# A conditioned transformer block on one core: the last two attention runs cut into four, gelu in chunks at the end, the residual of the last tile by an identity matmul, and Q projections asked for one group earlier

## The chip, the cores and the metric

The kernel runs on one core of a Trainium2 chip. The metric is device time in microseconds (us), from the start of the program on that core to its end. Five engines work from queues of their own: TensorE (PE: matmuls, PEld: its weight loads), VectorE (DVE), ScalarE (ACT), GpSimd (POOL) and SyncE (SP, which here issues nearly all DMAs). An engine executes its queue in order; between engines there are only semaphores.

## The reference

What is computed, with B = 1, S = 2048 tokens, D = 512, 32 heads of 16, F = 1376, all tensors bf16:

```python
mod = (_silu(c) @ w_mod).reshape(c.shape[0], 6, 1, -1)
sa, ca, ga, sb, cb, gb = (mod[:, 0], ..., mod[:, 5])
h = _layernorm(x) * (1 + ca) + sa
qkv = (h @ wqkv).reshape(B, S, 3, H, Dh)          # q, k, v per head
p = softmax(q @ k^T * Dh ** (-0.5))
x = x + ga * ((p @ v).reshape(B, S, D) @ wo)
h = _layernorm(x) * (1 + cb) + sb
x = x + gb * (gelu_tanh(h @ w1 + b1) @ w2 + b2)
```

## The kernel before

**Tiling.** The 2048 tokens are four query blocks of 512 (`QB`), each of four 128-token tiles. Attention is done in 32 runs (`runs`, `NR`). A run takes four heads side by side and one query block of 512 columns; in the last block (`LAST`) a run takes eight heads and one half of the block, so that 256 columns of two heads stand beside each other. In a run the 16 key tiles of 128 are gone through; one key tile and one of the four head rows make a unit of 128 x 512 scores.

**Two ways to an exponential.** The score matmuls (`qk`, L856) contract over 32 rows and run side by side in row tiles of the PE array. For 12 of the 16 key tiles of a run the exponential is taken by ScalarE (L905), on groups of three and two units in turn (`SPAN = (3, 2)`, so 1536 and 1024 columns). For the other four (`DKS`) VectorE writes the score as an integer that is read as a bf16 (L946), with four shifted copies of it (L962, L978; pieces of the last copy are done by GpSimd, L984), and the five readings are averaged by weighted V. The product with V (`pv_op`, L1044) runs in column tiles of 32 and accumulates a run in one PSUM bank `od`; one row of V is a constant, so the softmax denominator comes with it.

**Order.** Nothing is scheduled on the chip. A list scheduler in the kernel file (`Plan`) gives each operation a duration, priorities (`dyn`) and due times, and writes out each engine's queue in the order that its own clock gives. Small differences between priorities come from a table `SEEDS`, one number for each 25 us of that clock. The order is fixed when the kernel is built.

**Around attention.** In front: x, `w_mod` and `wqkv` are loaded, `mod` for the first norm is made by matmuls with one column (L617, `mod_columns`), block 0 is normalised (`layer_norm`: `stats` on DVE, `rstd` on GpSimd, `apply` on DVE), transposed (L694) and modulated (L657 on ACT, L660 on DVE), then Q, K and V of the first heads are projected (`make_q`, `make_k`, `make_v`). Later Q groups are projected when the scores of the run before them are built (`want_q`, called in `qk_deps`); their rows are spread by eight small DMAs (`qm<-qs`, L763). After each run `normalise` copies `od` to SBUF, sends the denominators through DRAM and multiplies. After the last run of a block `block_tail` does the output projection (`wo_mm`), the second norm, the two matrices of the MLP and the store. ScalarE's gelu needs another table than its exponential, so each block's gelu stands between two table loads.

**The end.** Tiles 0 and 1 of the last block have their first MLP matrix done while the last runs go on; their gelu (L1281) waits until the last exponential is done (`finished`). Tiles 2 and 3 are finished by `last_half` after the last run: division on chip by two 32x32 transposes (L1336 to L1343), output projection, residual (L1353), norm, transposes (L1369), first matrix (L1381), gelu straight from PSUM (L1384), second matrix (L1210), sum (L1396), store.

## Time and profile before

| | us |
|---|---|
| median of 3 runs | 783.46 |
| lowest, highest | 781.15, 783.68 |
| the profiled execution: span from first to last instruction | 782.9 |

The profile's only time for its execution is this span; it lies 0.56 us below the median and inside the three runs. The page gives each engine's busy time, the chain of work that ended last, and groups of instructions by source line. A group is named by its line, engine and operation, with what it writes and reads; "x313" is a count. Timeline rows give start, duration, engine, line, operation, tiles and count, and in brackets the engine's idle time before it and what ended it. Window rows give, for a stretch of time, the busy time of PE, PEld, DVE, ACT and POOL, then the granted clock of PE as a share of full speed, the share of the DMA engines that was busy, and GB/s. A busy PE counts the latency of its matmuls (a 512-column matmul shows 0.38 us, though the next one starts after 0.22 us).

### The profile page before, as it was taken

To read this page: it belongs to the slowest core of one execution; us is meant where nothing else is said; L and a number is where in the kernel's file an instruction comes from. 1 tells how busy PE (TensorE), PEld (TensorE's weight loads), DVE (VectorE), ACT (ScalarE), POOL (GpSimd) and SP (SyncE) were. 2 spreads that over 40 slices of the span, in tenths; PEclk is the share of its full clock that TensorE was granted. 3 is DMA by queue.
4 is the path that set the end of the run, shared out by engine and by line. 5 is a ranking of instruction groups with operands and counts; after the bars stand their busy time and mean duration, and the time that the engine had idled before them with its cause. 6 is when DMAs were issued, how large, how long until landed. Compare 5 with 4: busy or idle time off the path is not lost.

```text
span 782.9 us, 20900 instructions
## 1 busy us (share of the span) xinstructions
PE 730.8 (93%) x8315; PEld 271.3 (35%) x8395; DVE 722.6 (92%) x1269; ACT 752.0 (96%) x677; POOL 256.6 (33%) x492
## 2 busy tenths in 40 slices
PE   8889999999999999999999999999999999999997
PEld 3323333233333222233223233332333444444444
DVE  6789989999999999999999999999987999998984
ACT  4999999999999999999999999999999999999994
POOL 6620434333352534231313134234202432142320
PEclk9999999999999999999999999999999999999999
DMA  7043001100002001000101000000110000100000
GB/s 216 28 147 83 18 23 43 27 23 5 17 21 75 25 17 49 17 13 15 47 19 30 29 19 17 20 22 19 29 57 24 23 22 18 46 25 18 25 18 28
DMA packets 38547, 27.71 MB, mean 35 GB/s; under 512 B 17941, under 2 KB 33846, under 8 KB 38450
## 3 DMA queue, kind: packets, MB, share of 16 engines
q1 hardware_dynamic: 38442, 26.39, 11.8%
q8 instruction: 65, 1.06, 0.5%
q14 instruction: 32, 0.26, 0.1%
q10 hardware_dynamic: 8, 0.00, 0.0%
HBM read 20.77 MB, written 2.61 MB: 30 GB/s over the span
## 4 chain that ended last, share of the span: by engine, by line
ACT 37%; PE 34%; DVE 16%; issue 10%; DMA 2%; POOL 1%; SPq 0%; DVEq 0%; POOLq 0%; ACTq 0%
ACT pt L905 35%; PE od L1044 12%; PE st L856 10%; DVE ph L946 7%; DVE sh L962 4%; PE ax L1210 4%; PE ax L1271 3%; PE ax L856 2%; PE ax L735 1%; DMA blk<-in_w_mod_dram 1%; ACT g L1286 1%; PE t L1381 1%; DVE sh L978 1%; PE od L481 1%; DVE g L1276 1%
## 5 line engine op out<-in xcount | busy, mean ns | idle before, releaser
L905 ACT ACTIVATE pt<-st 128x1536 bf16<-128x1536 f32 x626 | 710.7, 1325 | 7.6 <-PE st L856 3.8
L946 DVE TENSOR_SCALAR ph<-ax 128x512 int16<-128x512 f32 x484 | 315.8, 681 | 25.3 <-PE ax L856 23.1
L856 PE MATMUL st<-qm,kT 32*128 32x512 bf16 x1564 | 246.4, 384 | 26.7 <-ACT pt L905 19.9
L962 DVE TENSOR_SCALAR sh<-ph 128x2048 int16<-128x2048 int16 x363 | 242.4, 700 | 2.0 <-PE od L1044 1.2
L984 POOL TENSOR_TENSOR sh<-ph,pair_sh 128x256 int32<-128x256 int32 x212 | 128.8, 616 | 280.6 <-DVE sh L962 190.4
L1044 PE MATMUL od<-sh,VX 128*32 128x512 bf16 (+1 forms) x2432 | 172.5, 342 | 1.7 <-DVE sh L962 0.7
L856 PE MATMUL ax<-qm,kT 32*128 32x512 bf16 x484 | 165.2, 380 | 7.3 <-DVE ph L946 4.3
L856 PEld LDWEIGHTS <-kT 32*128 32x128 bf16 x2048 | 79.4, 91 | 240.6 <-issue 228.7
L1044 PE MATMUL od<-pt,VEB 128*32 128x512 bf16 (+1 forms) x1952 | 142.7, 342 | 0.7 <-DVE OD L1069 0.5
L1044 PEld LDWEIGHTS <-VX 128*32 128x32 bf16 x2432 | 60.2, 96 | 82.7 <-issue 71.6
L1044 PEld LDWEIGHTS <-VEB 128*32 128x32 bf16 x2560 | 62.9, 96 | 73.5 <-issue 58.9
L1096 POOL TENSOR_TENSOR OT<-OD,RB 128x256 bf16<-128x256 f32 x38 | 29.0, 774 | 72.7 <-DVE sh L962 60.1
L978 DVE TENSOR_SCALAR sh<-ph 128x2048 int16<-128x2048 int16 (+3 forms) x86 | 50.7, 594 | 0.4 <-PE od L1044 0.3
L1044 PE MATMUL od<-ph,VEB 128*32 128x512 bf16 (+1 forms) x608 | 48.5, 341 | 0.4 <-DVE OD L1069 0.4
L1271 PE MATMUL ax<-blk,W 128*128 128x512 bf16 (+1 forms) x155 | 41.5, 352 | 1.7 <-issue 0.5
L1096 POOL TENSOR_TENSOR OS<-OD,RB 128x256 bf16<-128x256 f32 x24 | 17.5, 741 | 63.2 <-DVE sh L962 26.0
L790 POOL TENSOR_SCALAR VX<-VEB 128x128 bf16<-128x128 bf16 x64 | 23.4, 366 | 38.0 <-DVE VEB L667 34.8
L1210 PE MATMUL ax<-w,g 128*128 128x512 bf16 x115 | 32.4, 381 | 2.2 <-ACT g L1281 1.1
L735 PE MATMUL ax<-blk,w 128*128 128x512 bf16 x93 | 30.9, 383 | 2.8 <-ACT blk L657 0.6
L1276 DVE TENSOR_SCALAR g<-ax,b1c 128x512 bf16<-128x512 f32 (+1 forms) x44 | 29.3, 678 | 0.2
L641 DVE BATCH_NORM_STATS2 ln_s<-xb 128x6 f32<-128x512 bf16 x32 | 21.7, 678 | 1.8 <-DMA xb<-in_A_x_dram 1.7
L1210 PEld LDWEIGHTS <-g 128*128 128x128 bf16 x176 | 14.1, 97 | 24.5 <-issue 11.9
(109 smaller groups left out, 407.5 us busy)
## 6 DMA issues: line engine op xcount, KB each, us to landing
RB<-rn SPq DMA_DIRECT2D x124, 64.0 KB
xb<-in_A_x_dram SPq DMA_DIRECT2D x7, 512.0 KB
out_dram<-o SPq DMA_DIRECT2D x16, 128.0 KB
qm<-qs SPq DMA_DIRECT2D x120, 16.0 KB
W<-in_B_w_dram SPq DMA_DIRECT2D x1, 1376.0 KB
w<-in_A_wqkv_dram SPq DMA_DIRECT2D x3, 384.0 KB
blk<-in_w_mod_dram SPq DMA_DIRECT2D x2, 512.0 KB
g<-in_w_mod_dram SPq DMA_DIRECT2D x2, 512.0 KB
```

What stands on the lines that cost most here:

```text
L735: return chain([(lambda ps, j=j: nc.tensor.matmul(out=ps[:, 0:QB], lhsT=w.tile[:, j, cc * P:(cc + 1) * P], rhs=o_h[b].tile[:, j, :], start ...
L856: nc.tensor.matmul(out=o.tile[:, k * QB:(k + 1) * QB], lhsT=kT[cc][kb][rows, ko * P:(ko + 1) * P], rhs=qm.tile[rows, par, :] if hb is None ...
L905: nc.scalar.activation(out=e.tile[:, 0:len(got) * QB], in_=o.tile[:, 0:len(got) * QB], func=ACT.Exp, scale=ESC)
L946: nc.vector.tensor_scalar(out=ph.tile[:, o.row * QB:(o.row + 1) * QB], in0=o.tile, scalar1=PH_B, scalar2=0.0, op0=ALU.add, op1=ALU.max)
L962: sh = op("DVE", lambda o, j=j: nc.vector.tensor_scalar(out=o.tile, in0=first.tile, scalar1=PH_SH[j], scalar2=None, op0=ALU.add), 0.6, es, ...
L978: return nc.vector.tensor_scalar(out=sh.tile[:, at], in0=first.tile[:, at], scalar1=PH_SH[-1], scalar2=None, op0=ALU.add)
L984: return nc.gpsimd.tensor_tensor(out=sh.tile[:, at].bitcast(I32), in0=first.tile[:, at].bitcast(I32), in1=pair_sh[:, 0:1].to_broadcast([P, ...
L1044: nc.tensor.matmul(out=o_od[r].tile[32 * i:32 * i + 32, n * HB:n * HB + w], lhsT=v_tile(kt, ph)[:, c0:c0 + 32], rhs=got[i][:, at:at + w], ...
L1096: two = beside(lambda c: nc.gpsimd.tensor_tensor(out=OT.tile[:, c], in0=OD.tile[:, c], in1=o5.tile[:, c], op=ALU.mult), (OT,), (OD, o5), f ...
L1210: nc.tensor.matmul(out=ps, lhsT=g[:, f, col:col + P], rhs=rhs, start=(f == 0), stop=(f == NF - 1))
L1271: mm = chain([(lambda ps, f=f, j=j, f0=f0: nc.tensor.matmul(out=ps[:, (f - f0) * N:(f - f0 + 1) * N], lhsT=W1[:, j, f * P:(f + 1) * P], rh ...
L1276: ev.append(op("DVE", lambda o, f=f, f0=f0, mm=mm: nc.vector.tensor_scalar(out=g.tile[:, f, 0:N], in0=mm.tile[:, (f - f0) * N:(f - f0 + 1) ...
```

## The change

- **Loads.** `x` is taken with four consecutive tokens in a partition, `w_mod`'s first two parts are loaded in four row quarters, and the first `wqkv` load waits for the second quarter instead of the first half. The loads' sizes and priorities in the scheduler are changed.
- **First norm.** A function of its own, `first_norm`: `mod` accumulates quarter by quarter (`first_mod`) and is evicted by one DVE addition; the 128x512 modulations become 128x256 halves, DVE and ACT each taking two of the four feature chunks. K of blocks 0 and 1 is projected in two pieces (`split_k`), the first 128 columns by themselves. The epsilon of early norms is added on DVE.
- **Q.** `want_q` is called with one group more.
- **Last runs.** The runs of heads 6 and 7 of the last block are each split by query tile: four runs of 128 queries (`tile_of`), in which a unit is two key tiles by two heads by 128 queries. Score matmuls of these have 256 columns, V matmuls 128.
- **End.** Tile 2 is finished by `last_tile` while the last run goes on, up to its first matrix; its gelu comes after the last exponential, as one instruction. Tile 3 is finished by `last_last`: x enters the PSUM bank by a matmul with the identity, the norm reads PSUM, and the second matrix is done in two halves of 256 columns, each stored for itself. Tiles 0 and 1: evictions of several feature chunks in one DVE instruction (`evict_g`), gelu in four chunks (`PARTS`) instead of two. A constant row replaces a memset of ones for `b2`.
- **Scheduler.** Another `SEEDS` table, read every 12.5 us; other due times (`TAIL2`, `TAIL3`).

```diff
-SEEDS = (327, 149, ...)
+SEEDS = (105, 215, ...)
+STRETCH = 12.5
...
-    TAIL2, TAIL3 = 148, 95
+    TAIL2, TAIL3 = 115, 50
...
-    x_src = A_x[0].rearrange("(b t p) d -> b p t d", t=TPB, p=P)
+    x_src = A_x[0].rearrange("(b p t) d -> b p t d", t=TPB, p=P)
...
-    def load_mod(i):
+    def load_mod(j):
         def go(o):
-            first[i] = nc.sync.dma_start(out=o.tile, in_=wm_src[:, :, i * D:(i + 1) * D])
-        return dma(go, kb=512, acq=r_blk, prio=0.01 + 0.01 * i)
-    o_wm = {i: load_mod(i) for i in (0, 1)}
+            first[j] = nc.sync.dma_start(out=mod_cols(j), in_=wm_src[:, j, 0:2 * D])
+        return dma(go, (o_mod,), kb=250, prio=0.2 * j - 4.6)
+    o_wm = {j: load_mod(j) for j in range(NC)}
...
-            if lo == 0 and i == 0:
-                behind(0, got)
+            if (lo, i) == (0, 0):
+                behind(1, got)
...
+    def split_k(b, kind):
+        evs = []
+        for lo, hi in ((0, P), (P, QB)):
+            mm = chain([(lambda ps, j=j, lo=lo, hi=hi: nc.tensor.matmul(
+                out=ps[:, 0:hi - lo], lhsT=o_w[1].tile[:, j, 0:P], rhs=o_h[b].tile[:, j, lo:hi],
+                start=(j == 0), stop=(j == NC - 1)), MM * (hi - lo) / QB) for j in range(NC)],
+                [o_w[1], o_w0[1]], kind, r_ax, (o_h[b], o_w[1]), need=lambda j: o_hd[b][j])
...
-    runs = [...] + [(LAST, u) for u in range(8)]
+    runs = [...] + [(LAST, u) for u in range(6)] + 2 * [(LAST, 6), (LAST, 7)]
+    tile_of = {NR - 4: 2, NR - 3: 2, NR - 2: 3, NR - 1: 3}
...
-        want_q(r // 2 + 1 if r < LAST * 8 else r - LAST * 4 + 2)
+        want_q(r // 2 + 2 if r < LAST * 8 else r - LAST * 4 + 3)
...
+            w = QB // (1 if hb is None else 2 * len(kt))
+            parts = [(k, p) for k in kt for p in ((par,) if hb is None else (0, 1))]
+            for n, (k, p) in enumerate(parts):
                 for i in range(4):
                     c0 = VW * (8 * cc + 2 * i + p)
-                    w = QB if hb is None else HB
-                    at = n * HB
...
+                                     lhsT=v_tile(k, ph)[:, c0:c0 + 32],
+                                     rhs=got[i][:, n * w:(n + 1) * w], start=first and hb is None,
...
+    def evict_g(g, fs, lo, n, mm, prio=0.3):
+        return op("DVE", lambda o: nc.vector.tensor_tensor(
+            out=g.tile[:, fs[0]:fs[0] + len(fs), lo:lo + n],
+            in0=mm.tile[:, 0:len(fs) * n].rearrange("p (f q) -> p f q", f=len(fs)),
+            in1=b1c[:, fs[0]:fs[0] + len(fs)].unsqueeze(2).to_broadcast([P, len(fs), n]), op=ALU.add),
...
+    def last_last(r, t, OT, x2):
...
+        def residual(o):
+            nc.tensor.matmul(out=acc.tile, lhsT=ident, rhs=x2.tile[:, t, :], start=True, stop=False)
+            wo_mm(acc.tile, b, t, 0, 3, True)
...
+        ml = quick(r, OT)
+        w = op("PE", lambda o: [wo_last(acc.tile, t, p) for p in range(2)], 2 * MM, (ml, early), ...)
+        st = op("DVE", lambda o: (stats(ln, t, acc.tile), plus_eps(nc.vector, ln, t, t + 1)), 1.0, (w, ln), prio=0.022)
+        rs = op("POOL", lambda o: rstd(ln, t, t + 1, True), 0.8, (st,), prio=0.0)
+        za = op("DVE", lambda o: apply(ln, z, t, acc.tile), 0.6, (rs, z), prio=0.021, rel=(acc,))
+        xa = op("DVE", lambda o: nc.vector.tensor_copy(out=x2.tile[:, t, :], in_=acc.tile), 0.6, (w,), prio=0.2, ...)
...
+        for c in (slice(0, HB), slice(HB, D)):
+            first = prev = None
+            for f in range(NF):
...
+            dma(lambda o, c=c: nc.sync.dma_start(out=out_dst[b, t][:, c], in_=out_t.tile[:, c]), (a,), kb=64)
```

509 lines of the change are left out of this document (320 added, 189 removed).

## The prediction

> **What bounds the kernel now.** I read the page first, then ScalarE's groups with shapes kept apart, then windows, and then the timeline of the two ends.
>
> ```profile
> span 782.9 us, 20900 instructions
> PE 730.8 (93%) x8315; PEld 271.3 (35%) x8395; DVE 722.6 (92%) x1269; ACT 752.0 (96%) x677; POOL 256.6 (33%) x492
> ACT 37%; PE 34%; DVE 16%; issue 10%; DMA 2%; POOL 1%; SPq 0%; DVEq 0%; POOLq 0%; ACTq 0%
> ...
> L905 ACT ACTIVATE pt<-st 128x1536 bf16<-128x1536 f32 x313 | 481.5, 1538 | 3.6 <-PE st L856 2.5 <-PE ax L856 0.8
> L905 ACT ACTIVATE pt<-st 128x1024 bf16<-128x1024 f32 x312 | 347.5, 1114 | 4.0 <-PE ax L856 2.5 <-PE st L856 1.2
> ...
> 300.00:325.00 25.00, 22.31 (x233) 6.23 (x230) 22.12 (x38) 22.79 (x21) 7.54 (x12) 0.86 0.07 18
> 575.00:600.00 25.00, 23.63 (x354) 9.98 (x356) 17.82 (x30) 24.16 (x22) 2.89 (x4) 1.00 0.17 52
> 717.00:760.00 43.00, 41.96 (x701) 20.69 (x703) 40.73 (x72) 42.94 (x39) 15.31 (x21) 1.00 0.09 23
> ```
>
> The chain of waits shares out nearly evenly between ACT and PE, but the groups say which of them has no room: 625 exponentials cover the span from the first to the last of them, and all the idle time ahead of them is 3.6 + 4.0 = 7.6 us. Between those two moments the kernel is bound by ScalarE, and the change takes no exponential away: after it there are 313 of 1536, 312 of 1024 and one of 512 columns again, and three full gelus. So the middle can give back a few us of idle time at most. Its larger holes are two windows: 2.2 us at 300 to 325, where the granted clock of PE is 0.86, and 0.84 us at 575 to 600. In the last 43 us ACT idles 0.06 us, and PE and DVE are nearly full too. What can be gained lies ahead of the first exponential and behind the last one.
>
> ```profile
> 7.00:8.00 1.00, 0.62 (x16) 0.34 (x14) 0.60 (x2) 0.00 (x0) 0.92 (x3) 1.00 0.40 141
> 8.00:9.00 1.00, 0.67 (x11) 0.17 (x7) 0.79 (x2) 0.00 (x0) 0.94 (x5) 1.00 0.24 65
> ...
> 7.63 1.47 SPq L555 DMA_DIRECT2D w<-in_A_wqkv_dram  x3
> 8.21 0.90 DVE L652 TENSOR_SCALAR z<-xb,mv,rs 128x512 bf16<-128x512 bf16 x2 [0.61 <-POOL rs L648]
> 9.08 0.55 PE L617 MATMUL ax<-sc,blk 128*128 128x1 bf16 x16 [0.41 <-DMA blk<-in_w_mod_dram]
> 9.67 0.17 DVE L630 COPY modA<-ax 128x8 f32<-128x8 f32 x1 [0.56 <-PE ax L617]
> 9.87 0.18 DVE L631 TENSOR_SCALAR modA<-modA 128x4 f32<-128x4 f32 x1
> 10.36 1.00 DVE L660 TENSOR_SCALAR blk<-st,modA 128x512 bf16<-128x512 bf16 x2 [0.31 <-PE st L694]
> 10.94 1.45 ACT L657 ACTIVATE blk<-st,modA 128x512 bf16<-128x512 bf16 x2 [4.20 <-DVE blk L660]
> 12.85 1.41 DVE L753 TENSOR_SCALAR qm<-st,qmask 128x512 bf16<-128x512 f32 x2 [1.49 <-PE st L735]
> 13.71 0.59 ACT L665 CAST kT<-ax 128x512 bf16<-128x512 f32 x1 [1.33 <-PE ax L735]
> 14.79 4.62 ACT L905 ACTIVATE pt<-st 128x1536 bf16<-128x1536 f32 x4 [0.49 <-PE st L856]
> ```
>
> **The front** is a single file: the second half of `w_mod` (PE starts at 9.08), `modA` at 10.05, modulation by DVE and then by ACT to 12.39, Q, its mask, K, scores, and the first exponential at 14.79. Between 7 and 9 us the DMAs move only 141 and 65 GB/s, since `wqkv` is asked for at 7.63.
>
> ```profile
> 760.01 1.28 ACT L1281 ACT_TABLE_LOAD   x1
> 760.04 0.38 PE L1044 MATMUL od<-pt,VEB 128*32 128x256 bf16 x5 [0.20 <-ACT pt L905]
> 760.46 0.45 DVE L1336 STREAM_TRANSPOSE OD<-od 128x256 f32<-128x256 f32 x1 [1.93 <-PE od L1044]
> 761.66 0.42 DVE L1343 TENSOR_TENSOR OT<-od,OD 128x256 bf16<-128x256 f32 x1
> 763.13 0.69 DVE L1353 TENSOR_TENSOR xb<-t,xb 128x512 bf16<-128x512 f32 x1
> 765.77 0.41 DVE L652 TENSOR_SCALAR z<-xb,mv,rs 128x512 bf16<-128x512 bf16 x1 [0.70 <-POOL rs L648]
> 766.91 0.59 DVE L660 TENSOR_SCALAR blk<-t,modB 128x128 bf16<-128x128 bf16 x2
> 767.08 0.81 ACT L657 ACTIVATE blk<-t,modB 128x128 bf16<-128x128 bf16 x2 [3.14 <-PE t L1369]
> 768.98 1.95 PE L1381 MATMUL t<-blk,W 128*128 128x128 bf16 x32
> 769.40 2.18 ACT L1384 ACTIVATE g<-t,b1c 128x128 bf16<-128x128 f32 x8 [1.51 <-PE t L1381]
> 772.11 3.71 ACT L1384 ACTIVATE g<-t,b1c 128x128 bf16<-128x128 f32 x14
> 772.28 2.69 PE L1381 MATMUL t<-blk,W 128*128 128x128 bf16 x44
> 776.76 1.89 PE L1210 MATMUL ax<-w,g 128*128 128x512 bf16 x8
> 779.33 0.69 DVE L1396 TENSOR_TENSOR o<-ax,xb 128x512 bf16<-128x512 f32 x1 [1.68 <-PE ax L1210]
> ```
>
> **The tail** lasts from the last exponential at 760.01 to 782.9: 22.9 us. Two tiles share it, so that PE, from 762 on, is never free for long: the second tile's first matrix (772.28) stands behind the first tile's, and the second matrix closes the file at 779.3.
>
> **Front, by steps.** `wqkv` now waits for the second of four quarters, so the hole at 7 to 9 us closes and weights stand ready; x and the quarters ahead of them on SP's queue are the same bytes. `w_mod` is complete between 8.0 (all bytes moved without a hole) and 9.1; I take 9.05, as before. Then 8 one-column matmuls (half of 0.55) instead of 16, one DVE operation (0.17) instead of two: `modA` at about 9.65, 0.4 earlier. The modulation is four 256-column pieces on each of two engines at once. ACT's 1.45 for two of 512 and 0.81 for two of 128 put one of 256 near 0.5, so ACT ends at 9.75 + 2.1 = 11.85 instead of 12.39. Q follows as before (12.39 to 12.85: 0.46), one mask of 0.7 (half of 1.41) until 13.0; the 128 columns of K are copied beside it, where the 0.59 copy of 512 ended at 14.30. Scores take 0.45 (14.30 + 0.04 to 14.79): first exponential at 13.45, or 1.35 earlier; with `w_mod` at 8.0 it is 2.4. In the opposite case, no better modulation, only `modA`'s 0.4 is left. I take 1.5 (0.4 to 2.4).
>
> **Tail, by steps,** from the last exponential E. The order in which the built kernel stands gives the queues.
> 1. Division: before E + 2.07 (761.66 + 0.42). Now two evictions of tile 2 stand on DVE between the reciprocal and the second transpose: 512 columns from PSUM at 0.69 (the L1353 row) and 384, some 0.58. OT at E + 3.34.
> 2. Output projection: as before 1.05 (762.08 to 763.13), E + 4.4.
> 3. From there to z it was 2.64 (763.13 to 765.77). The residual addition (0.69) is now a matmul that runs before the division is done; epsilon moves from POOL to DVE, which I count as even. But DVE copies the sum (0.69, while POOL works) and adds tile 0's output ahead of z: I add 0.35 of that 0.69. z starts at E + 6.7, and reads fp32 from PSUM at 0.69 (L1353 again) instead of 0.41: E + 7.4.
> 4. Transposes and modulation: 0.73 and 0.98 (766.18 to 767.89), E + 9.1.
> 5. First matrix and gelu: 0.42 to the first gelu, then 11 x 0.265 (3.71 / 14): E + 12.5. Tile 2's gelu stands ahead of these on ACT and is done long before.
> 6. PE then has one chain of eleven 256-column matmuls to do, at half of 1.89 / 8: 1.2. Behind it in PE's queue stand eight 512-column ones, the rest of tile 2's second matrix: 1.89. E + 15.7, sum 0.69, and the store 2.9 (782.9 less 780.02): E + 19.3.
>
> So the tail is 3.6 shorter. If the rest of tile 2 and the evictions fit beside other work, 6; if PE comes late to E, 1.5.
>
> **Middle, by steps.**
>
> ```profile
> 25.00:50.00 25.00, 21.41 (x210) 9.14 (x214) 18.64 (x37) 23.97 (x24) 12.70 (x50) 1.00 0.20 64
> 308.00:310.00 2.00, 2.00 (x22) 0.51 (x20) 1.46 (x3) 1.67 (x2) 0.00 (x0) 0.50 0.31 76
> ...
> 588.75 3.23 DMA qm<-qs
> ...
> 737.07 0.62 PE L1044 MATMUL od<-pt,VEB 128*32 128x256 bf16 x16
> ...
> L1044 PE MATMUL od<-sh,VX 128*32 128x256 bf16 x256 | 10.9, 275 | 0.0
> L1276 DVE TENSOR_SCALAR g<-ax,b1c 128x256 bf16<-128x256 f32 x11 | 4.8, 477 | 0.1
> ```
>
> *Q a group earlier* is worth the wait for `qm` at 588, where ACT lost 0.84: take -0.8. The projection, one DVE eviction and eight DMAs move past a run's work on PE, DVE and SP's queue; behind them on SP are `normalise`'s DMAs, which have a whole run before anybody needs them. If that cover is thin, the 0.8 comes back elsewhere: 0 to -0.8.
>
> *Start-up.* ACT idles 1.03 us between 25 and 50, while the later blocks are normed. The closed DMA hole brings them earlier, and K of block 1 in pieces lets scores start: -0.5 (0 to -1), against +0.2 on ACT for one copy more (0.59 for 512 columns, 128 apart from 384).
>
> *The V matmuls of 128 columns* have no row. Sixteen of 256 columns take 0.62; without one latency of 0.275 that is 0.345 for three further rounds of four column tiles, 0.108 a round (half of the 0.216 of 512 columns) and some 0.02 for the last round's four starts, so neighbours start about 7 ns apart. By the built programs, 512 matmuls of 256 (128 rounds, 13.8 us) give way to 960 of 128, 240 rounds. If the columns set the pace, a round is 0.054 and the sum 13.0: nothing is lost. If a round stays at 0.108, it is 25.9: +12. Four starts 7 ns apart fit into 0.054, so I am near the low end: +1.0. The score matmuls, two of 256 for one of 512, stream the same columns.
>
> The Trainium skill speaks against it: TensorE: Matmul & The Clock Gate, section "Wait — 56ns, not 53.3ns?", has a floor under the spacing of matmuls, about 25 ns from start to start however few the columns. By it the 960 would take 24 us, 10 more than the 13.8 before. The row's 7 ns between neighbours in different column tiles disagrees with it, so I leave it to a rival.
>
> *DVE and PE in the last 43 us.* Tile 2's division, residual, norm, modulation and evictions come in ahead of E: 1.6 (E + 0.45 to 2.07, four operations) + 0.69 + 0.7 + 0.41 + 4 x 0.3 + 1.8 = 6.4, and a second quick division costs 0.8 over the copy that it replaces; eviction in groups saves 11 x 0.48 less 5 x 0.69 and one 0.48, so 1.3. DVE has 43 - 40.73 = 2.3 free there. It may work ahead on its key tiles, and had 7.2 us free at 575 to 600: I take +0.5 (0 to 3.6, which is 6.4 + 0.8 - 1.3 - 2.3). What would be late next are the integer exponentials, then V matmuls of the run, then the buffers that ACT writes.
>
> The rest of the edits (identity matmul early, constant row, smaller memsets, `SEEDS`) I cost at nothing in themselves; POOL, idle for two thirds of the span, covers its part. What `SEEDS` reshuffles is the idle time: the 2.2 us at 300 to 325 come from PE at half clock (0.50 at 308 to 310), and such a place may vanish or appear: -2.2 to +2.5, taken 0.
>
> Sum against the profiled span: 782.9 - 1.5 - 3.6 - 0.8 - 0.5 + 0.2 + 1.0 + 0.5 = **778.2**. The span is 0.56 below the median of the runs, inside their 2.5 us of scatter, so I leave the figure as it is.
>
> **Rivals.**
> *The middle gains too:* PE's clock stays up and the 2.2 us of 300 to 325 go as well: 776.0, and with the front's and tail's better bounds down to 773. For it: ACT's 7.6 us of idle time are nearly all in few places. Against: fewer warming matmuls stand in the new program (148 instead of 192 in `od`).
> *The 128-column matmuls are bound by issue* (slower). Place: the four last runs. ACT has 0.06 us free there, so what PE loses, ACT loses. It decides from the point at which the sum passes 785.8: 7.6 more than forecast, 8.6 more than the 13.8 before, 22.4 over 960, or 23 ns a matmul. At 27 ns (0.108 a round) it is 778.2 - 1.0 + 12.1 = 789.3. For it: nothing in the trace is as short; against: the 7 ns. At the skill's 25 ns it would be about 787.
> *The tail doesn't shrink as said.* W2 of three tiles still waits for the last exponential's table change, 33 x 0.216 = 7.1 us of PE work; if PE comes to tile 3's division late, only 1.5 is won: 780.3.
> *DVE becomes the bound* in the last 43 us: +3.6 instead of +0.5, 781.3. For it: 40.73 of 43 busy. Against: its work can be drawn forward.
>
> **How the numbers follow.** Forecast 0.45, its own range 775.5 to 780.7; middle gains 0.20; tail 0.12; DVE 0.13; issue 0.10. About 0.3% (2.35 us around 783.46) is what a measurement can tell from no change: faster means below 781.1, slower above 785.8. The forecast is faster except for a small part (0.44 of 0.45), the gaining middle 0.20, the tail rival in two thirds (0.08), DVE in half (0.05): 0.77 faster. Same: 0.13. Slower: 0.10. The range, 773.0 to 783.5, leaves out the issue-bound case and the far ends.
>
> **What would show it.** Front: first exponential near 13.4, `wqkv` issued before 7, no dip of the DMA at 7 to 9. Middle: no wait for `qm` near 590; V matmuls of 128 columns, sixteen in about 0.40 us (three rounds of 0.054, 0.02, and a latency of 0.22); if instead sixteen still take 0.6 and ACT idles in the last two runs' place, the issue rival holds. Tail: 19.3 us from the gelu's table load to the end, closed by tile 2's sum on DVE (L1471), after tile 3's two stores. The prediction is wrong if ACT's idle time between its first and last exponential grows by more than 3 us, or if the tail stays above 21.5.

## The result, and the profile after

| | before | after |
|---|---|---|
| median of 20 runs, us | 783.33 | 780.60 |
| lowest, highest | 781.07, 785.23 | 778.91, 783.50 |
| after to before | | 0.9969 (95%: 0.9959 to 0.9979) |
| profiled execution: span, time | 782.9, not given | 778.5, 780.36 |

The change makes the kernel 0.31% faster, 2.4 to 2.7 us. The forecast was 5.3 (from 783.46 to 778.2). In all later executions, where span and time are both listed, the time is the span plus 1.7 to 2.1 us. One run of the kernel before beside the later experiments took 1029.07 us at a mean clock of 0.556 and is left out.

I read the profile after in the three parts of the prediction. First the page and the windows that answer to those shown of before (PE, PEld, DVE, ACT, POOL busy, then PE's clock, DMA share, GB/s):

```profile
span 778.5 us, 22044 instructions
PE 726.3 (93%) x8886; PEld 274.8 (35%) x8964; DVE 725.6 (93%) x1294; ACT 751.3 (97%) x671; POOL 242.1 (31%) x466
```

```profile
7.00:8.00 1.00, 1.00 (x11) 0.42 (x11) 0.92 (x5) 0.00 (x0) 0.90 (x2) 1.00 0.25 92
8.00:9.00 1.00, 1.00 (x11) 0.52 (x10) 0.51 (x2) 0.00 (x0) 0.22 (x1) 1.00 0.79 180
300.00:325.00 25.00, 23.36 (x240) 7.43 (x241) 24.93 (x47) 25.00 (x23) 4.76 (x8) 1.00 0.07 20
575.00:600.00 25.00, 21.30 (x376) 9.91 (x374) 22.46 (x41) 22.53 (x21) 5.61 (x9) 1.00 0.12 32
717.00:760.00 43.00, 41.39 (x1255) 25.82 (x1244) 39.10 (x77) 42.34 (x39) 9.32 (x15) 1.00 0.07 19
```

The dip of the DMA at 7 to 9 has moved rather than closed: 92 and 180 GB/s, before 141 and 65. The half clock at 300 to 325 is gone (ACT 25.00 of 25), but at 575 to 600, where an earlier Q was to save 0.84, ACT now idles 25.00 - 22.53 = 2.47. The timeline of both ends of the kernel after:

```profile
9.08 0.40 PE L675 MATMUL ax<-sc,g 128*128 128x1 bf16 x8
9.34 0.94 PE L811 MATMUL st<-ident,z 128*128 128x128 bf16 x8
9.52 0.17 DVE L798 TENSOR_TENSOR modA<-ax,plus 128x8 f32<-128x8 f32 x1 [1.01 <-PE ax L675]
9.60 0.40 DVE L698 TENSOR_SCALAR z<-xb,mv,rs 128x512 bf16<-128x512 bf16 x1
11.39 0.38 PE L811 MATMUL st<-ident,z 128*128 128x128 bf16 x4 [0.57 <-ACT blk L703]
11.81 1.02 ACT L703 ACTIVATE blk<-st,modA 128x256 bf16<-128x256 bf16 x2 [0.47 <-PE st L811]
14.56 1.45 ACT L1022 ACTIVATE pt<-st 128x1536 bf16<-128x1536 f32 x1 [0.76 <-PE st L974]
...
758.84 0.63 PE L1162 MATMUL od<-sh,VX 128*32 128x128 bf16 x32
759.30 0.89 PE L1162 MATMUL od<-pt,VEB 128*32 128x128 bf16 x48
759.78 1.28 ACT L1412 ACT_TABLE_LOAD   x1
760.13 1.18 PE L1500 MATMUL ax<-blk,W 128*128 128x128 bf16 x18
...
774.17 0.81 PE L1335 MATMUL ax<-W2c,g 128*128 128x512 bf16 x3
775.02 0.69 DVE L1471 TENSOR_TENSOR o<-ax,xb 128x512 bf16<-128x512 f32 x1 [1.23 <-PE ax L1335]
```

Front: the first exponential is at 14.56 (before 14.79, forecast 13.45), so 0.23 came of 1.5. Middle, from the first exponential to gelu's table load: 759.78 - 14.56 = 745.22, and before 760.01 - 14.79 = 745.22, the same. Tail: 778.5 - 759.78 = 18.72 (before 22.89, forecast 19.3), so 4.17 came of 3.6. The V matmuls of 128 columns take 0.63 for 32 and 0.89 for 48: 0.26 for four more rounds of four, 0.065 a round. That is nearer to the pace of the columns (0.054) than to 0.108, and 16 ns a matmul, where the rival "bound by issue" needs 23: it is out by this profile alone.

So the three parts of the two profiled executions differ by 4.4, close to the 4.7 of my sum. The medians differ by 2.7. Three questions follow: is the execution that I summed against a typical one; why did the front and the earlier Q give nothing; and what bounds the tail.

### The profile page after: what moved, and what is told of

Read it like the earlier page. It is cut to its first block, busy times and chain, and to the rows that moved or that the text cites. A ratio compares the mean times of both kernels' runs of the same rounds, so it can differ in the third digit from the quotient of the medians.

```text
span 778.5 us, 22044 instructions
## 1 busy us (share of the span) xinstructions
PE 726.3 (93%) x8886; PEld 274.8 (35%) x8964; DVE 725.6 (93%) x1294; ACT 751.3 (97%) x671; POOL 242.1 (31%) x466
## 4 chain that ended last, share of the span: by engine, by line
ACT 36%; PE 27%; DVE 22%; issue 11%; DMA 2%; POOL 1%; SPq 0%; DVEq 0%; POOLq 0%; ACTq 0%
ACT pt L1022 35%; DVE ph L1063 10%; PE od L1162 8%; PE st L974 7%; DVE sh L1079 6%; PE ax L1335 3%; PE ax L974 2%; PE ax L1400 2%; DVE ln_s L681 2%; PE ax L833 1%; DMA dc<-dn 1%; DVE sh L1095 1%; DVE OD L1201 1%; PE ax L1329 1%; ACT g L1417 1%
## 5 line engine op out<-in xcount | busy, mean ns | idle before, releaser
L974 PE MATMUL st<-qm,kT 32*128 32x512 bf16 (+1 forms) x1664 | 246.1, 370 | 21.0 <-ACT pt L1022 15.7
L1101 POOL TENSOR_TENSOR sh<-ph,pair_sh 128x256 int32<-128x256 int32 x198 | 119.4, 611 | 286.5 <-DVE sh L1079 184.6
L974 PE MATMUL ax<-qm,kT 32*128 32x512 bf16 (+1 forms) x512 | 169.8, 367 | 9.5 <-DVE ph L1063 5.8
L1162 PE MATMUL od<-sh,VX 128*32 128x512 bf16 (+2 forms) x2640 | 171.5, 327 | 2.7 <-DVE sh L1079 2.0
L1162 PE MATMUL od<-pt,VEB 128*32 128x512 bf16 (+2 forms) x2156 | 141.6, 324 | 0.8 <-ACT pt L1022 0.3
L1162 PEld LDWEIGHTS <-VEB 128*32 128x32 bf16 x2816 | 65.4, 96 | 70.3 <-issue 56.1
L1095 DVE TENSOR_SCALAR sh<-ph 128x2048 int16<-128x2048 int16 (+3 forms) x95 | 52.8, 563 | 0.3
L1228 POOL TENSOR_TENSOR OT<-OD,RB 128x256 bf16<-128x256 f32 x37 | 27.2, 745 | 75.2 <-DVE sh L1079 58.1
L1162 PE MATMUL od<-ph,VEB 128*32 128x512 bf16 (+2 forms) x660 | 48.2, 326 | 0.7 <-DVE OD L1201 0.7
L1228 POOL TENSOR_TENSOR OS<-OD,RB 128x256 bf16<-128x256 f32 x24 | 17.3, 728 | 42.0 <-DVE sh L1079 23.6
L1407 DVE TENSOR_SCALAR g<-ax,b1c 128x512 bf16<-128x512 f32 x33 | 24.5, 744 | 0.2
```

What stands on the lines that cost most here:

```text
L974: nc.tensor.matmul(out=o.tile[:, k * QB + n * w:k * QB + (n + 1) * w], lhsT=kT[cc][kb][rows, ko * P:(ko + 1) * P], rhs=qm.tile[rows, par, ...
L1095: return nc.vector.tensor_scalar(out=sh.tile[:, at], in0=first.tile[:, at], scalar1=PH_SH[-1], scalar2=None, op0=ALU.add)
L1101: return nc.gpsimd.tensor_tensor(out=sh.tile[:, at].bitcast(I32), in0=first.tile[:, at].bitcast(I32), in1=pair_sh[:, 0:1].to_broadcast([P, ...
L1162: nc.tensor.matmul(out=o_od[r].tile[32 * i:32 * i + 32, to:to + w], lhsT=v_tile(k, ph)[:, c0:c0 + 32], rhs=got[i][:, n * w:(n + 1) * w], s ...
L1228: two = beside(lambda c: nc.gpsimd.tensor_tensor(out=both_heads(OT.tile, tile_of[r]) if r in tile_of else OT.tile[:, c], in0=OD.tile[:, c] ...
```

## Experiments

Ratios are to the kernel before on the same chip. The numbers that were measured stand in one table ahead of the runs; "front", "middle" and "tail" are cut as above, "idle" is ACT's idle time in the middle, "to 25" is the first exponential's time plus ACT's idle time from there to 25 us, which shows how early the work behind the front gets going.

| kernel (one profiled execution) | span | clock | front | middle | idle | tail | to 25 | median time | ratio (95%) |
|---|---|---|---|---|---|---|---|---|---|
| before | 782.9 | 0.993 | 14.79 | 745.22 | 8.12 | 22.89 | 16.13 | 783.33 | 1 |
| b_look | 782.1 | 0.993 | 15.12 | 744.14 | 7.43 | 22.84 | 16.09 | 784.14, one run | |
| b_look2 | 779.2 | 1.000 | 14.51 | 741.86 | 5.13 | 22.83 | 15.58 | 780.99, one run | |
| before_q | 782.3 | 1.000 | 15.22 | 744.27 | 4.33 | 22.81 | 16.45 | 784.90 | 1.0023 (1.0011 to 1.0035) |
| before_seeds | 786.9 | 0.993 | 16.53 | 747.43 | 6.11 | 22.94 | 16.79 | 788.48 | 1.0052 (1.0032 to 1.0072) |
| after | 778.5 | 1.000 | 14.56 | 745.22 | 7.12 | 18.72 | 16.05 | 780.60 | 0.9969 (0.9959 to 0.9979) |
| after_look | 778.9 | 0.996 | 13.13 | 747.00 | 8.75 | 18.77 | 15.78 | 780.64, one run | |
| q_back | 798.1 | 0.976 | 13.97 | 761.98 | 19.27 | 22.15 | 14.55 | 796.62 | 1.0153 (1.0106 to 1.0201) |
| q_lead | 781.5 | 0.998 | 13.30 | 749.00 | 10.40 | 19.20 | 16.09 | 782.76 | 0.9993 (0.9979 to 1.0006) |
| z_first | 778.9 | 0.998 | 13.43 | 746.75 | 7.29 | 18.72 | 15.90 | 780.16 | 0.9968 (0.9954 to 0.9982) |
| w1_late | 778.9 | 0.996 | 14.16 | 744.71 | 6.38 | 20.03 | 15.97 | 781.45 | 0.9987 (0.9971 to 1.0002) |
| seeds_old | 786.6 | 0.991 | 13.00 | 751.56 | 11.14 | 22.04 | 15.82 | 789.01 | 1.0068 (1.0040 to 1.0096) |
| v_twice | 780.7 | 0.998 | 15.20 | 746.78 | 8.65 | 18.72 | 16.31 | 782.49, one run | |
| wq_first | 776.1 | 1.000 | 13.10 | 744.26 | 6.34 | 18.74 | 14.90 | 780.86 | 0.9969 (0.9950 to 0.9989) |
| qm_act | 776.0 | 0.995 | 13.92 | 743.30 | 5.31 | 18.78 | 15.73 | 777.93 | 0.9929 (0.9915 to 0.9944) |
| qm_wq | 777.6 | 0.996 | 14.00 | 744.88 | 6.69 | 18.72 | 15.93 | 778.31 | 0.9945 (0.9932 to 0.9957) |
| gelu_two | 777.5 | 1.000 | 14.31 | 744.15 | 6.40 | 19.04 | 16.04 | 781.54 | 0.9984 (0.9972 to 0.9996) |

**Was the profiled execution of before typical?** The kernel before, unchanged, twice more.

> The kernel before, profiled once more. Theory (the base was read wrongly): the time of an execution is its span and about 1.9 us more, and the first profiled execution held two stretches of half clock (307.5 to 311 and 318 to 321.4) that a usual one need not hold. Then this one has ACT idle below 1 us in the window 300 to 325 (it was 2.2), the middle, from the first exponential to gelu's table load, is 743.5 to 745 long instead of 745.22, and span plus 1.9 lies near the median of 783.3. Rival (the half clock belongs to the kernel's order of work): the same window is at half clock again, ACT idles 2 us or more there, and the middle is 745.2 again.

> The kernel before, profiled a third time. Theory (the two profiles so far each held one stretch of half clock in the middle that cost ACT about 2 us, at 308 and at 49 to 57, and an execution without it is that much shorter): with a mean clock of 0.997 or more, ACT idles 5 to 6 us between first and last exponential instead of 8.1 and 7.4, and the middle is 742 to 743.2 long, 2 to 3 shorter than the 745.22 of the kernel after. Rival (the middle of the kernel before is 744 to 745 in any case, and its executions differ at the ends): middle over 744 at a clock of 0.997 or more.

The first of the two has the signs of the theory (ACT has no idle time at 300 to 325, and the middle is 744.14 long), but it is not free of half clock, and in all it idles nearly as much as the first profile. The first profile has half clock from 307.6 to 311.0 (two microseconds of it stand in the prediction), from 317.8 to 321.2 and from 17.4 to 20.8; in b_look it had moved to the stretch from 47.7 to 58.0, which begins so:

```profile
46.00:48.00 2.00, 1.20 (x18) 0.36 (x11) 1.97 (x3) 2.00 (x3) 1.46 (x4) 0.93 1.03 341
48.00:50.00 2.00, 1.94 (x15) 0.27 (x15) 2.00 (x5) 0.72 (x2) 0.00 (x0) 0.50 1.04 343
50.00:52.00 2.00, 2.00 (x21) 0.59 (x23) 1.01 (x2) 1.20 (x1) 0.00 (x0) 0.50 0.05 16
```

The second held none between its first and its last exponential. Its whole middle in one window:

```profile
14.51:756.37 741.86, 696.19 (x8069) 255.02 (x8145) 702.84 (x1223) 736.72 (x642) 243.56 (x444) 1.00 0.11 32
```

At clock 1.00 the middle of before is 741.86, 3.36 shorter than in the profile that I had. The 79 runs of before that are left beside these experiments, on four chips whose averages agree to 0.3, say the same: at a mean clock of 0.993 they take 784.78 on average (11 runs), at 0.997 782.65 (22), at 1.000 781.41 (12). So the half clock belongs to an execution and not to one place in this kernel's order, and 3.4 us lie between a mean clock of 0.993 and one of 1.000. The rival is refuted. The three runs of the kernel after at 1.000 took 779.26, 779.70 and 780.36, on average 779.77: there the change is worth 1.6. With some half clock, at 0.993 to 0.998, the averages are 783.20 (63 runs of before) and 780.65 (15 of after): there it is worth 2.6.

**The earlier Q, by whole orders.** q_back is the kernel after with Q asked for when the kernel before asks for it:

```diff
-        want_q(r // 2 + 2 if r < LAST * 8 else r - LAST * 4 + 3)
+        want_q(r // 2 + 1 if r < LAST * 8 else r - LAST * 4 + 2)
...
-            due(32 + APR * (first_run(q_made[0]) - 1) - 48)
+            due(32 + APR * (first_run(q_made[0]) - 1) - 32)
```

before_q makes the reverse edit in the kernel before. q_lead is the kernel after with more lead in the last block:

```diff
-            due(32 + APR * (first_run(q_made[0]) - 1) - 48)
+            due(32 + APR * (first_run(q_made[0]) - 1) - (80 if first_run(q_made[0]) >= LAST * 8 else 48))
```

seeds_old is the kernel after with the tie numbers of before, and before_seeds the reverse:

```diff
-SEEDS = (105, 215, 995, ...)
+SEEDS = (327, 149, 358, ...)
-STRETCH = 12.5
+STRETCH = 25.0
```

> The kernel after, with Q made at the time at which the kernel before makes it (one group, one sixteenth-step later). Theory (Q a group earlier made the wait of 2.14 us for qm near 580): ACT's idle time at 575 to 600 falls from 2.47 to 0.5 to 1.0, and the span from 778.5 to about 777. Rival one (my prediction's step was right, the earlier Q is worth 0.8, and the wait at 580 comes from the reshuffled order): the wait for qm stays or another takes its place, and the span is 779 or more. Rival two (any reordering moves the same 2 to 3 us of idle time about): the sum of ACT's idle time between first and last exponential stays within 0.5 of that of the kernel after, wherever it lies.

> The kernel after, where the groups of Q for the last block are made still earlier in the order of work (32 units of a run's time more lead). Theory (the lead is what is short: the rows of qm are issued on SP at 573.98 to 579.22, between the rows of the norm that wait for one another, and the transfer of 2 to 3 us lands too late): no wait for qm of over 0.3 near 580, ACT's idle time at 575 to 600 under 1, span about 776.5. Rival (the place on SP's queue decides, not the lead): the wait comes back at another group of Q, with ACT idle 1.5 us or more there, and the span is 778 to 780.

> The kernel before with one part of the change alone: Q one group ahead. My prediction's step: the wait for qm near 588 goes, 0.8 us faster, ratio 0.999, ACT's idle time at 575 to 600 under 0.3. Theory (an earlier Q meets the DMAs of the norm on SP's queue): a wait for qm of 1 to 2.5 us near 575 to 600, and 1 to 2 us slower. Rival (where the idle time lies follows the order of work, which any edit redraws): idle time between first and last exponential of 5.5 to 10 in other windows than before, and a ratio between 0.997 and 1.003 that has nothing to do with qm.

> The kernel after with the numbers that order equal claims taken from the kernel before, and nothing else. Theory (2.5 us of ACT's idle time, at 575 to 600, is what this order of work costs, and another order has it elsewhere): the window 575 to 600 has under 1.5 us, other windows have 1 to 4, the sum of idle time between first and last exponential is 6 to 10 instead of 7.1, span 777 to 782. Rival (the numbers were chosen for the new program and are worth much): over 12 us of idle time and a span of 785 or more. Front and tail: as after, within 0.5, apart from the front's 13.3 to 14.6.

> The kernel before with the numbers that order equal claims taken from the kernel after, and nothing else. Theory (each list fits the program that it stands in, and is worth several us to it: with the old list the kernel after was 1% slower): 3 to 9 us slower, ratio 1.004 to 1.012, by exponentials moved to ACT (over 626), by idle time of 10 or more, or by a later division in the tail. Rival (the old list is simply the worse one): 0 to 3 us faster than before.

Against expectation, q_back is 1.5% slower than before and nothing about the wait can be read from its time: the scheduler wrote another order from end to end, with four windows of 25 us at a clock of 0.73 to 0.93, and 19.27 of idle time in all. q_lead has no wait at 575 to 600 (0.14), but new idle time, 2.59 and 1.57 in the two windows from 700 to 750, and is slower than after. before_q does what my step said where it said it: against the clean execution of before, idle time at 575 to 600 goes from 0.92 to 0.07, and in all from 5.13 to 4.33, which is the 0.8 of the forecast. It is slower all the same, since its order gives ScalarE 629 exponentials instead of 626. ACT's busy time in the middle, fourth of the engines:

```profile
15.22:759.49 744.27, 703.55 (x8084) 256.56 (x8084) 696.10 (x1215) 739.95 (x645) 233.79 (x432) 1.00 0.12 32
```

739.95 against 736.72 in the clean execution of before, 3.2 more. The tables of tie numbers matter by as much: the kernel after with the old table is 1.0% slower than with its own (1.0068 to 0.9969), the kernel before with the new one 0.5% slower. In seeds_old, DVE is still at its own exponentials when ScalarE is done, so that the last tile's division starts 6.3 us behind the table load instead of 0.45, and the tail is 22.04 long. Each table fits its program and is worth 4 to 8 us there. I had costed it at nothing: a single edit of a program that is ordered this way can't be judged by its time alone, only by its place in the trace or by an edit that leaves the order as it is.

**The wait near 580, with the order left as it is.** after_look first, to see whether it comes back.

> The kernel after, profiled once more. Theory (the wait near 580 belongs to the order of work, while the front varies from execution to execution): ACT idles 2.2 to 2.7 in the window 575 to 600 again, the middle from first exponential to gelu's table load is 744.5 to 746 long, the tail 18.6 to 18.9, and the first exponential starts where the landing of the last quarter of w_mod and PE's granted clock put it, 13.3 to 14.6. Rival (the wait at 580 is an accident of one execution, as the half clock at 300 to 325 was for the kernel before): under 1 us of idle time at 575 to 600.

It does: 3.36 of idle time (with half clock behind the wait, from 581.8 to 585.2), 2.01 in w1_late and 1.78 in wq_first, whose orders are the same there. SP's queue and PE in the kernel after show why:

```profile
573.26 0.69 DVE L869 TENSOR_SCALAR qs<-ax 128x512 bf16<-128x512 f32 x1
...
573.98 0.55 SPq L875 DMA_DIRECT2D qm<-qs  x1
...
574.63 1.37 SPq L1209 DMA_DIRECT2D dc<-dn  x1
...
576.09 2.45 SPq L875 DMA_DIRECT2D qm<-qs  x4
...
578.64 0.53 SPq L1217 DMA_DIRECT2D rn<-dc  x1
...
579.22 1.77 SPq L875 DMA_DIRECT2D qm<-qs  x3
...
581.70 0.37 PE L974 MATMUL ax<-qm,kT 32*128 32x512 bf16 x1 [2.14 <-DMA qm<-qs]
```

Q's rows are ready at 573.95, but SP issues the last three at 579.22, behind `dc` and `rn` of a `normalise`, each of which waits for the transfer or the reciprocal before it. qm_act issues these eight rows from ACT's queue; PE's, DVE's and POOL's instructions and ACT's others keep their places.

```diff
-                rows = [dma(lambda o, at=slice(i, i + 16), p=p: nc.sync.dma_start(
+                rows = [dma(lambda o, at=slice(i, i + 16), p=p: (nc.scalar if (b, cc) == groups[13] else nc.sync).dma_start(
```

> The kernel after, where the eight rows of qm of the fourteenth group of Q (the one waited for near 580) are issued on ACT's queue instead of SP's; no other instruction changes its place. Theory (the wait of 2.14 us comes from SP's queue, where seven of the eight rows stand behind the transfers of a norm that wait for one another: issues at 573.98, 576.09 and 579.22): the rows land before 579, no wait for qm of over 0.3 there, ACT's idle time at 575 to 600 falls from 2.0 to 3.4 (three executions) to under 0.8, and the time falls by 1.5 to 2.5 against the kernel after, less some 0.5 that eight issues cost ACT: 778.5 to 779.5, ratio about 0.995. Rival (something else is late by as much at that place, the norm's own rows for one): the idle time stays over 1.5, or moves to the next 25 us, and the time stays at 780 to 781.

```profile
572.81 0.68 DVE L869 TENSOR_SCALAR qs<-ax 128x512 bf16<-128x512 f32 x1
573.45 0.32 SPq L1209 DMA_DIRECT2D dc<-dn  x1
573.57 0.61 ACTq L875 DMA_DIRECT2D qm<-qs  x1
574.36 0.69 ACTq L875 DMA_DIRECT2D qm<-qs  x1
575.23 1.15 ACTq L875 DMA_DIRECT2D qm<-qs  x2
```

```profile
575.00:600.00 25.00, 23.24 (x403) 10.76 (x395) 24.14 (x42) 24.52 (x23) 5.62 (x9) 1.00 0.12 31
```

ACT's idle time there falls from 2.47 to 0.48, and the median is 777.93 (ratio 0.9929, where after has 0.9969). The theory holds, and the gain is a little above its range: runs at clock 1.000 average 777.68 (three) against 779.77. This is the fastest of all the kernels here.

**The front.** z_first holds modA's last quarter until the first two transposes and z of the fourth tile stand ahead of it on PE and DVE:

```diff
-                    [o_mod], 1, lambda j: o_wm[j])
+                    [o_mod], 1, lambda j: o_wm[j] if j < NC - 1 else op("NIL", None, 0.0, (o_wm[j], trs[0], trs[1], za[3]), lat=0.0, prio=0.0))
```

> The kernel after, with the last quarter of modA held behind the first pair of transposes and behind z of the fourth tile, so that these stand ahead of it on PE and on DVE. Theory (the front was lost to the order in the queues, since the transposes started at 9.34 behind modA's last matmuls and z of tile 3 at 9.60 behind modA): ACT's modulation ends near 11.9 instead of 12.83 and the first exponential starts at 13.6 to 13.9 instead of 14.56. Rival (the loads and the first norm set the front): z of the fourth tile comes at 9 or later whatever stands in the queue, modA is only pushed back, and the first exponential starts at 14.4 to 14.9. The span is read at the first exponential, since the order behind it may be another.

wq_first loads Q's other columns of `wqkv` ahead of K's and V's (and the index that goes with the list):

```diff
-        o_w1[b - 1] = load_cols((1, 2, 0)[b - 1], P, D, 0.5 * b - 2.7)
+        o_w1[b - 1] = load_cols((0, 1, 2)[b - 1], P, D, 0.5 * b - 2.7)
```

> The kernel after, where the rest of Q's columns of wqkv is loaded ahead of the rest of K's and V's instead of behind them; no other instruction changes its place. Theory (the front's gain is given back at once, since the Q that is now made a group ahead stands on PE's queue and waits for its columns, which land last, at 17.3 to 18.2, whenever the first exponential starts): the first exponential stays at 13.0 to 14.6, PE has no wait for wqkv at 17 to 18, and the first exponential's time plus ACT's idle time up to 25 falls from 15.8 to 16.1 (six executions of the kernel after and its variants) to 14.5 to 15.1; no half clock at 18 to 22; the time falls by 0.8 to 1.3, to 779.3 to 779.8. Rival (the next transfer takes its place: K's or V's columns or x of a later block, late by what Q's columns gain): the sum at 25 us falls, but ACT's idle time at 25 to 75 grows by as much, and the time stays.

v_twice does the sixteen matmuls of the first V twice, in `make_v`:

```diff
-            for j in range(NC):
+            for j in [*range(NC)] * (2 if (b, cc) == (0, 0) else 1):
```

> The kernel after, where the sixteen matmuls of the first V are done twice, which adds 0.95 us of PE work at about 15 us, ahead of its wait for Q's columns. Theory (the half clock at 18.2 to 22, seen in three of four executions whose first exponential starts before 13.5, follows the hole that PE has at 15 to 17.6, where it is busy 33 to 57%): no half clock at 18 to 22, and ACT's idle time up to 25 is 1.3 to 2.0 with a first exponential at 13.0 to 13.5, against 2.5 to 2.8. Rival (the half clock follows the wait for the columns itself or the load of PE before it): clock 0.5 at 19 to 21 again, idle time 2.5 or more.

The front of one and the same kernel varies by 1.4 (14.56 in after, 13.13 in after_look), with the speed of PE in the first microseconds. A warming matmul of 512 columns takes 0.59 to 0.64 in after until 9 us, as it does at half clock (0.63 at 308 in the first profile of before), although the window rows give the clock there as 1.00; in after_look it takes 0.38 from 6 us on. The kernels with after's order in front fall into two groups by this. With 0.38 from 6 us on, the first exponential starts at 13.00 to 13.30 (seeds_old, wq_first, after_look, q_lead), which is where the forecast had it (13.45); with 0.59 to 0.64 in some of the time before it, at 13.92 to 15.20 (qm_act, q_back, qm_wq, w1_late, gelu_two, after, v_twice). The two executions of before with 0.38 from 5 us on have it at 14.51 and 14.79.

z_first had 0.38 too and starts at 13.43, later than all of the first group. From the start of modA to the first exponential it takes 4.10, where after_look takes 4.72, after 5.04 and the clean execution of before 5.13; but modA itself comes at 9.33, in after_look at 8.41. With the transposes and z ahead, the way behind modA is shorter, as the theory said, but modA is pushed back by more, as the rival said, and nothing is gained. What the front lost in the profile of after is PE's speed.

The gain does not last, though. The column "to 25" is 15.7 to 16.1 in nearly every kernel with the earlier Q, however early the first exponential comes. In after_look and wq_first:

```profile
17.61 1.04 PE L833 MATMUL ax<-blk,w 128*128 128x512 bf16 x4 [0.72 <-DMA w<-in_A_wqkv_dram]
18.69 0.69 DVE L869 TENSOR_SCALAR qs<-ax 128x512 bf16<-128x512 f32 x1 [0.53 <-PE ax L833]
19.24 1.45 ACT L1022 ACTIVATE pt<-st 128x1536 bf16<-128x1536 f32 x1 [0.53 <-PE st L974]
```

```profile
15.39 5.54 ACT L1022 ACTIVATE pt<-st 128x1024 bf16<-128x1024 f32 x5 [0.48 <-PE st L974]
16.79 0.55 PEld L833 LDWEIGHTS <-w 128*128 128x128 bf16 x4 [0.23 <-issue]
16.79 1.04 PE L833 MATMUL ax<-blk,w 128*128 128x512 bf16 x4
```

Q of a later group now stands on PE's queue ahead of the scores and, when the first exponential is early, waits for its columns, which land last, at 17.3 to 18.2. With these columns loaded first the wait is gone, five exponentials run without a break, and "to 25" is 14.90, as expected. In q_back, where Q is not asked for earlier, it does not stand there, and "to 25" is 14.55. The median does not show it (780.86): three of the nine runs had clock 1.000 and took 777.88 to 779.11, the other six 0.989 to 0.996 and 780.26 to 782.88. v_twice tells nothing: its first exponential came at 15.20, so the condition to be tested was not met.

qm_wq has both queue edits.

> The kernel after with both queue edits: the eight rows of qm of the fourteenth group on ACT's queue, and Q's columns of wqkv loaded ahead of K's and V's. Theory (the two waits are independent places): in an execution at clock 1.0, 777.9 less 1.1 gives 776.5 to 777, idle time between first and last exponential 4.5 to 5, and the median is 776.5 to 778. Rival (the earlier start-up brings half clock, as the nine executions with the columns first had 0.989 to 0.996 in six): median 778 to 779.5 with most clocks under 0.997, no better than the rows on ACT's queue alone.

The rival describes it better: 778.31 is no better than the rows alone (the intervals overlap). Four of its five runs did have a mean clock of 1.000, so half clock in mid-kernel is not the reason; the mean says little of the first 10 us (it is 1.000 in after). In the profiled run PE was at half clock from 7.6 to 11.0, the first exponential came at 14.00, PE had nothing to wait for at 17.7 either way, and "to 25" is 15.93. What an early start is worth over many executions stays open.

**The tail.** w1_late holds tile 2's first matrix until the last exponential is done:

```diff
+        late = op("NIL", None, 0.0, (), lat=0.0, prio=0.0, gate=finished)
...
-                hd + [o_late["w1"], g], kind, r_ax, (h,), len(fs))
+                hd + [o_late["w1"], g, late], kind, r_ax, (h,), len(fs))
```

> The kernel after, with the first matrix of tile 2 (the last but one) held until the last exponential is done, so that this PE work falls back into the tail. Theory (the tail is PE's queue: what left PE behind the last exponential is what the tail lost): 44 matmuls of 128 columns, 2.7 us by the kernel before, come back, the tail goes from 18.72 to 21.2 to 21.8 and the time up by 2 to 3. Rival (the tail is the last tile's own chain of division, norm, gelu, sum): PE has room beside it, the tail is 18.7 to 19.5, and the time is as after.

gelu_two makes two pieces of gelu out of four (and the index that goes with them). It is the gelu of tiles 0 and 1, which the expectation calls tile 2's; tile 2's own is one instruction in both kernels:

```diff
-    PARTS = ((0, 2), (2, 5), (5, 8), (8, 11))
+    PARTS = ((0, 2), (2, 11))
```

> The kernel after, with tile 2's gelu behind the last exponential in two pieces (two and nine blocks) instead of four; only the tail's order changes. Theory (PE bounds the tail, so whatever it has to do while it waits for gelu counts nothing): PE has 18 first-matrix matmuls, the identity and two projections, about 2.5 us, for the 2.9 of the larger piece, so PE waits 0.5 to 1.5 and the tail is 19.2 to 20.2 instead of 18.7 to 18.8. Rival (the pieces of gelu are not what feeds the tail): 18.6 to 19.0. If the chunks carry the whole gain of the tail: over 21.

The tail of w1_late is 20.03, 1.31 longer and not 2.7: in the kernel after 18 of the 44 matmuls stood behind the table load already (760.13 in the timeline above), in w1_late 40. The 22 more, at 2.62 / 44 = 0.0595 (a row of 44 takes 2.62), make 1.31. So every matmul that is put behind the last exponential lengthens the tail by its own duration: PE bounds it. From the table load to the last sum, in the kernels before, after and w1_late:

```profile
760.01:779.33 19.32, 17.96 (x152) 10.77 (x154) 9.91 (x23) 11.14 (x29) 1.60 (x4) 1.00 0.06 21
```

```profile
759.78:775.02 15.24, 15.10 (x153) 9.61 (x143) 7.54 (x17) 9.12 (x19) 0.55 (x1) 1.00 0.09 28
```

```profile
758.87:775.33 16.46, 16.46 (x166) 11.07 (x162) 8.13 (x19) 9.24 (x19) 0.55 (x1) 1.00 0.08 25
```

Of the 4.08 that the stretch lost, 17.96 - 15.10 = 2.86 is PE work that now lies ahead of the table load, and 1.36 - 0.14 = 1.22 is time in which PE waited. gelu_two gives 19.04, between the two ranges and 0.32 more than after; PE waits for the larger piece once:

```profile
762.45 1.47 PE L1335 MATMUL ax<-w,g 128*128 128x512 bf16 x6 [0.31 <-ACT g L1412]
```

## Why the forecast was too large

Direction and range were right, and the tail carried the gain as said. Its size was wrong by half, in these steps of the sum:

| step | forecast | against the profile I had | against the clean execution |
|---|---|---|---|
| front, to the first exponential | -1.5 | -0.23 | +0.05 (after_look: -1.38) |
| middle (-0.8 - 0.5 + 0.2 + 1.0 + 0.5) | +0.4 | 0.00 | +3.36 |
| tail | -3.6 | -4.17 | -4.11 |
| sum | -4.7 | -4.4 | -0.7 |

1. *"The span is 0.56 below the median of the runs, inside their 2.5 us of scatter, so I leave the figure as it is."* This step failed first. A span isn't a time: with 1.7 to 2.1 beside it, the profiled execution took some 784.8, 1.5 above the median of 783.33. And the 778.2 is a sum of spans that was given as a time: with 1.9 beside it, it is 780.1, 3.2 below that median. What the profiled execution had too much was in plain sight: the 2.2 us at half clock at 300 to 325, which I took as part of the kernel's order and costed at 0 for the change. It belonged to that execution. The sum against it came out nearly right (-4.4), but by luck, since the profile of after held no such stretch. The rival "the middle gains too" counted on these 2.2 us; they went, but they go in an execution of the kernel before as well.
2. *Q a group earlier, -0.8.* Of the middle's 3.36, idle time is 7.12 - 5.13 = 1.99, and of that the window 575 to 600 has 1.55 (2.47 against 0.92 in the clean execution of before). I looked for what stands behind Q's rows on SP's queue, "`normalise`'s DMAs, which have a whole run before anybody needs them". What decides is what stands ahead of them. qm_act removes it, 2.0 of idle time and 2.7 of the median (2.1 between runs at clock 1.000). That the earlier Q alone puts the rows there isn't shown: before_q and, in another order of work, z_first have it and no such wait (0.07 and 0.00 of idle time at 575 to 600).
3. *Front, -1.5.* With PE at full speed the sum comes out (13.00 to 13.30 against 14.51 and 14.79 before), but by two errors that nearly cancel. The last quarter of `w_mod` is in use from 7.8 to 8.2 on and not from 9.05, so that modA ends at 8.50 to 8.76 instead of 9.65; from there it takes 4.5 instead of 3.8, since z of the fourth tile and transposes stand behind modA (z_first, which has them ahead: 3.93). And the step did not ask for PE's speed: in the profile of after, with half of it until 9 us, modA ends at 9.69 and the rest takes 4.87. And the end of the front wasn't followed further: Q's columns land at 17.3 to 18.2 and take an early front back by 25 us. "To 25" is 16.05 and 15.78 in the two executions of after and 15.58 to 16.13 in the three of before: nothing is gained there.
4. *Start-up -0.5, K copy +0.2.* The start-up gained nothing: ACT idles 1.04 between 25 and 50, before 1.03. ACT's own work in the middle grew by 1.4, from 736.72 to

```profile
14.56:759.78 745.22, 699.32 (x8669) 259.92 (x8744) 709.10 (x1252) 738.12 (x645) 231.92 (x414) 1.00 0.12 32
```

   Its K copies account for 0.5 of that (2.4 against 1.9); the rest lies in 626 exponentials that overlap a little less, and no run takes it apart.
5. *The V matmuls +1.0, DVE +0.5.* In the last 43 us ACT idles 0.66 (before 0.06) and DVE has 3.9 free. The two rivals that stood on these, issue and DVE, are refuted; of the +1.5 at most 0.6 is there. The Trainium skill's page TensorE: Matmul & The Clock Gate, section "Wait — 56ns, not 53.3ns?", has a floor of about 25 ns between matmul starts; the rows above show 0.26 for 16 further ones, 16 ns each, so for neighbours in four column tiles the floor doesn't hold here.
6. *Tail -3.6.* Right, and 0.5 too small, because I followed the last tile's own chain and added the leftovers of tile 2 behind it (its last step but one, 12.5 + 1.2 + 1.89, makes 15.6 and not 15.7). PE's queue sets the end, and what left it sets the gain: 2.86 of work (tile 2's projection, transposes and 26 of the 44 matmuls of its first matrix) and 1.22 of waiting. The rival "the tail doesn't shrink as said" is refuted.

What the medians show, 2.7, lies between the two columns. Most executions of both kernels hold some half clock (67 of the 79 of before, 17 of the 20 of after), and it costs the kernel after less: 780.65 against 779.77, before 783.20 against 781.41. Why it costs less is open.

## What to carry to other kernels

Before summing against a profiled execution, place that execution among the runs by its time and its clock, and take out of it what belongs to that execution alone. For a step that is moved to an earlier place, read what then stands ahead of it on each queue, its weights' loads and the DMAs of others that wait for one another, and follow a gained microsecond at least to the next transfer that lands at a fixed time. Read the speed of PE in the first microseconds from the duration of a known matmul. Where an order is written out by a scheduler with tie numbers fitted to it, test an edit in a way that leaves the order as it is.

## What the runs showed of the hardware

In these profiles PE's clock falls to half for about 3.4 us or for two, three or four times that: 3.4 at 307.6 and 317.8 in the first profile of before, 6.8 from 122.9 in before_seeds, 10.3 from 47.7 in b_look, 13.6 from 53.9 in q_back. Several of these stretches follow one in which PE had little to do. In after_look PE is busy 39 to 40% from 15 to 18, then:

```profile
17.00:18.00 1.00, 0.39 (x2) 0.21 (x3) 0.93 (x5) 1.00 (x2) 0.78 (x4) 1.00 0.01 2
18.00:19.00 1.00, 1.00 (x7) 0.20 (x4) 0.47 (x2) 0.71 (x1) 0.91 (x7) 0.81 0.00 0
19.00:20.00 1.00, 1.00 (x11) 0.48 (x12) 1.00 (x3) 0.76 (x1) 0.98 (x3) 0.50 0.00 0
20.00:21.00 1.00, 1.00 (x12) 0.16 (x4) 1.00 (x2) 0.69 (x1) 0.94 (x4) 0.50 0.00 0
21.00:22.00 1.00, 1.00 (x10) 0.50 (x7) 0.93 (x4) 0.29 (x1) 0.40 (x1) 0.50 0.51 98
```

A share of 0.81 and three of 0.50 are 0.38 + 3 us at half speed. q_lead and z_first have the same hole and the same half clock there; wq_first, without the wait, has clock 1.00 throughout. That the hole is the cause was not shown on its own, since v_twice did not reach its condition, and a hole is neither enough nor needed. In after PE is busy 1.21 of 3.40 from 578.5 on and the clock stays at 1.00, while after_look, with 1.31 of 3.30 at the same place, has half clock behind it; and in seeds_old the half clock from 76.1 on follows 3.4 us in which PE was busy 3.17. The Trainium skill's page TensorE: Matmul & The Clock Gate, section "What's actually happening", has the clock set by how busy PE was in a window of about 3.4 us that runs freely and does not start anew with the kernel. The lengths here agree with it, and a freely running window would explain why the same order of work meets the half clock at 308, at 48 or not at all in three executions of the kernel before; the case in seeds_old it does not explain.
